# The second layer of 19 of 48 blocks as seven products of halves, two operand sums by accumulating DMA and two by VectorE

## The chip, the cores and the metric

The kernel runs on one core of a Trainium2 chip. Its time is the device time of one execution in microseconds (us), as a median over runs. One execution was also recorded by the hardware profiler; stretches and durations below come from that one.

## The reference

Two steps follow one another. First a filter along the sequence, in the frequency domain; then a two-layer network on every token, with a leaky activation whose slope for negative values is learned per hidden unit.

```python
# x: (8, 3008, 256); filt_r, filt_i: (1505, 256)
X = np.fft.rfft(x, axis=1)
Y = X * (filt_r + 1j * filt_i)[None]
y = np.fft.irfft(Y, n=3008, axis=1).reshape(24064, 256)
h = y @ w_in                                   # 256 -> 2048
g = np.maximum(h, 0.0) + alpha * np.minimum(h, 0.0)
out = g @ w_out                                # 2048 -> 256, float32
```

## The kernel before

**Blocks and steps.** The 24064 tokens are cut into 48 blocks: four times 12 blocks (two batches each), of which one has 384 tokens and the others 512. A block is worked in 16 steps, one for each tile of 128 hidden units. All engines are given their instructions in an order written out by hand; nothing is moved by a scheduler. Each engine takes its own instructions in that order and waits on semaphores for the others.

**First layer, `up(j)` (L446 to L456).** In step j TensorE multiplies two 128-row tiles of the transformed tokens `yT` by hidden tile j of `win_s`: two matmuls of 512 columns into PSUM tile `hps` (two buffers, each for a pair of hidden tiles). After each odd j ScalarE copies the pair as fp16 into `gtb` (L452), and VectorE makes the activation: two instructions `min(g, 0) * (alpha - 1)` into `m` (L455) and one sum `g + m` over the pair (L456). `gtb` is a ring of 17 pairs; a block fills eight.

**Second layer, `down(q)` (L465).** Beside the first layer of a block, TensorE does the second layer of the block before it: in each step a sixteenth of 64 matmuls, four of 256 columns, whose stationary operand is 128 hidden units x 128 tokens of `gtb` and whose moving operand is `wout_s`. 16 matmuls accumulate one tile of 128 tokens x 256 outputs in PSUM tile `op`; ScalarE evicts two of those at a time (L470) into `osb`, and SP's queue stores them. The last block is done by `finish` (L476), whose last 32 matmuls are 128 columns wide.

**The transform.** While a block of one batch is multiplied, the transform of a later batch is put between the steps in small pieces, by a plan that gives a step for each (`STEPS_A` to `STEPS_D`, in steps from the start of a batch's 96). `piece_a` is one matmul of 512 columns (L176); its result goes by `asb` to a DRAM scratch (`save_a`) and comes back turned (`turn_a`). `piece_b` (L196) has two matmuls of 256 columns, two multiplications by VectorE from PSUM (L199 `ww`, L200 `uu`), and two DMAs on POOL's queue that add `ww` into `uu` across the halves of the partitions (L202; `accum_op`). `piece_c` (L215) has two matmuls of 256 columns; its result `v` goes to DRAM (`turn_c`) and comes back as `zt`. `piece_d` has four matmuls of 94 columns into `yT` (L237). ScalarE evicts pieces a, c and d (L244). `BANKS` says which of two PSUM banks (`psF`) each piece takes. POOL's queue also loads x, with a cast from fp32 to fp16 (L138).

Batch 0 has a transform of its own at the start (`First`). The first 80 us hold it and the loading of the weights.

Of the kernel before, what the change touches and what calls it, by code (L numbers as in the profile page):

```python
# [16 lines left out]
NK1 = 24  # L17
# [6 lines left out]
    "010101010101010101010010101010101010110101010011001011101010010101011001010101010101010110101011"  # L24
    "001010110101010101010010010101010101010010101101010100110101010010101010101011011010101010101011"
    "010100101010110010101011010101010101001001010101010101001010110101010011010101001010101010101101"
    "10101010101010110101010101010101010101011010101010010101"
)
STEPS_A = (-84, -82, -74, -69, -67, -61, -59, -58, -55, -53, -52, -50, -47, -44, -41, -40)
STEPS_B = (-22, -16, -12, 1, 7, 16, 23, 29, 38, 45, 51, 56)  # L30
STEPS_C = (-1, 9, 20, 27, 34, 36, 42, 50, 54, 66, 70, 70)
STEPS_D = (89, 90, 90, 92, 93, 94, 96, 99, 101, 101, 103, 110, 114, 121, 127, 129)
# [44 lines left out]
def kernel(  # L77
# [22 lines left out]
    p_fft = ctx.enter_context(tc.tile_pool(name="p_fft", bufs=1))  # L100
    p_uw = ctx.enter_context(tc.tile_pool(name="p_uw", bufs=3))
# [3 lines left out]
    psO = ctx.enter_context(tc.tile_pool(name="psO", bufs=2, space=bass.MemoryType.PSUM))  # L105
# [21 lines left out]
    gtb = konst.tile([128, 17, 2, 512], FP16, name="gtb")  # L127
    twx_s = gtb[:, 14:17].rearrange("p a b c -> p (a b c)").rearrange("p (k m) -> p k m", m=128)
# [30 lines left out]

    class Fft:  # L160
        def __init__(self, b):
            self.b = b
            self.base = (b % 2) * NFFT
            self.px, self.uw = {}, {}

        def start_a(self):
            self.asb = p_fft.tile([96, NH, D], FP16, name="asb")
            self.at = p_fft.tile([128, NK1, D], FP16, name="at")

        def piece_a(self, i, evict, wide=False):  # L170
            if i == 0:
                self.start_a()
            xs = xc[(self.b, i // 4)]
            ps = bank(wide)
            o = (i % 4) * 512
            nc.tensor.matmul(ps[0:96], wf1_s, xs[:, o : o + 512], start=True, stop=True)  # L176
            evict(self.asb[:, 2 * i : 2 * i + 2].rearrange("p a d -> p (a d)"), ps[0:96])

        def save_a(self, c):
            s = slice(8 * c, 8 * c + 8)  # L180
            nc.sync.dma_start(out=a_dram[self.b, :, s], in_=self.asb[:, s])
# [23 lines left out]
        def piece_c(self, kp, evict, pv=None):  # L205
            if kp == 0:
                self.v = p_fft.tile([128, NK1, D], FP16, name="v")
                self.zt = p_fft.tile([96, NH, D], FP16, name="zt")
# [9 lines left out]
        def turn_c(self, q):  # L218
# [8 lines left out]
            if q == 3:  # L227
                for g in range(4):
                    s = slice(8 * g, 8 * g + 8)
                    nc.sync.dma_start(out=self.zt[:, s], in_=v_dram[self.b, :, s])  # L230

        def piece_d(self, i, evict, wide=False):
# [3 lines left out]
            for m in range(4):  # L236
                nc.tensor.matmul(ps[:, m], self.zt[:, 8 * g + 4 * mh + m, dh * 128 : dh * 128 + 128],  # L237
# [14 lines left out]
    class First(Fft):  # L252
        def __init__(self):
# [3 lines left out]
            self.zt = p_fft.tile([96, NH, D], FP16, name="zt")  # L257
            self.am = gtb[:, 0:6].rearrange("p a b c -> p (a b c)")
# [21 lines left out]
        def piece_b(self, kp):  # L280
# [6 lines left out]
            uw = gtb[:, 6 + kp % 8]  # L287
# [4 lines left out]
        def piece_c(self, kp, evict):  # L292
            uu, ww = self.uw.pop(kp)
            tw, tx = (t.rearrange("p k (q g e) -> p k g q e", q=4, e=4) for t in (twi_s, twx_s))
            pv = psO.tile([128, 2, D], FP32, name="op").rearrange("p k d -> p (k d)")
# [10 lines left out]
        def piece_t(self, i, evict, wide=False):  # L306
            pt = bank(wide)
            m = self.vm.rearrange("p (g m e) -> p g m e", m=96, e=4)
# [5 lines left out]
            evict(self.zt[:, 2 * i : 2 * i + 2].rearrange("p a d -> p (a d)"), pt[0:96])  # L314
# [34 lines left out]
    def warm(n):  # L349
        pw = psO.tile([128, 2, D], FP32, name="op")  # L350
# [12 lines left out]
    alp = psO.tile([128, 2, D], FP32, name="op")  # L363
# [70 lines left out]
    turn = [0]  # L434

    class Block:
        def __init__(self, p, t0, tn):
            self.p, self.t0, self.tn = p, t0, tn
            self.gts = []

        def up(self, j):
# [6 lines left out]
            if j % 2 == 1:  # L448
                g = gtb[:, turn[0] % 17]
                turn[0] += 1  # L450
                m = p_m.tile([128, 2, 512], FP16, name="m")
                nc.scalar.activation(g[:, :, 0:tn], self.hps[:, :, 0:tn], AF.Copy)  # L452
                for i in range(2):
                    a = alm_s[:, j - 1 + i : j + i]
                    nc.vector.tensor_scalar(m[:, i, 0:tn], g[:, i, 0:tn], 0.0, a, OP.min, OP.mult)  # L455
                nc.vector.tensor_add(g[:, :, 0:tn], g[:, :, 0:tn], m[:, :, 0:tn])  # L456
                self.gts += [g[:, 0], g[:, 1]]

        def down(self, q):
            n = self.tn // 128  # L460
            for w in range(n * q, n * (q + 1)):
                si, k = w // 16, w % 16
                if si % 2 == 0 and k == 0:
                    self.op = psO.tile([128, 2, D], FP32, name="op")
                nc.tensor.matmul(self.op[:, si % 2], self.gts[k][:, 128 * si : 128 * si + 128],  # L465
                                 wout_s[:, k], start=(k == 0), stop=(k == 15))
                if k == 15 and (si % 2 == 1 or si == n - 1):
                    m = si % 2 + 1
                    osb = p_osb.tile([128, 2, D], FP32, name="osb")
                    nc.scalar.activation(osb[:, 0:m], self.op[:, 0:m], AF.Copy)  # L470
                    for lane in range(m):
                        store(self.p, self.t0 + 128 * (si - m + 1 + lane), osb, lane)

        def finish(self):
            def down(acc, si, k, first, ca=0, cb=D):
                nc.tensor.matmul(acc, self.gts[k][:, 128 * si : 128 * si + 128], wout_s[:, k, ca:cb],  # L476
                                 start=first, stop=(k == 15), skip_group_check=True)

            op = psO.tile([128, 2, D], FP32, name="op")
# [11 lines left out]
            accs.insert(0, psO.tile([128, 2, D], FP32, name="op")[:, 0])  # L491
# [12 lines left out]
    def plan_fft(b, a0, ga, ta, b0, gap, add, lag, d0, quarters, x_at):  # L504
# [17 lines left out]
        for i in range(16):  # L522
            put(d0 + min(i, 4) + 2 * max(i - 4, 0), f.piece_d, i, on_act)

# [77 lines left out]
```

## Time and profile before

| | |
|---|---|
| median of 3 runs | 792.93 us (792.37 to 792.95) |
| the profiled execution's own time | 792.78 us |
| its span from first to last instruction | 791.0 us |
| TensorE matmuls (PE) | 772.4 us busy, 98% |
| VectorE (DVE) | 621.3 us, 79% |
| ScalarE (ACT) | 597.2 us, 76% |
| GpSimd (POOL) | 198.2 us, 25% |
| TensorE clock granted | 1.00 |
| DMA | 100.78 MB, 127 GB/s over the span |

The span is 1.8 us shorter than the execution's own time: what lies before the first and after the last instruction. Busy time of TensorE counts overlapping matmuls once; a matmul's duration contains its way through the array, so the pace of a stream is read from the distance of the starts. Engines are named as the profile names them: PE, PEld (weight loads), DVE, ACT, POOL and SP.

### The profile page before, as it was taken

The page shows a single profiled execution, that of the slowest core. Times are in us where ns is not written, and L with a number is a line of the kernel's source. Part 1 is how long each engine was busy: PE and PEld are TensorE (multiplying, and loading weights), DVE is VectorE, ACT ScalarE, POOL GpSimd, SP SyncE. Part 2 cuts the span into 40 slices and gives each one's busy share as a digit, 9 for nine tenths or more (in the row PEclk, how much of TensorE's full clock was granted, in tenths as well). Part 3 has the DMA queues.
Part 4 walks back from the last instruction along what each step waited for, and adds up shares of the span by engine and source line. Part 5 has one row for each costly group of instructions (what it writes and reads, how often), then busy time and mean ns, then how long its engine had stood idle before and what let it go on. Part 6 is the DMA issues. An engine that isn't in the chain of part 4 may idle for free.

```text
span 791.0 us, 16125 instructions
## 1 busy us (share of the span) xinstructions
PE 772.4 (98%) x5944; PEld 538.9 (68%) x5944; DVE 621.3 (79%) x1370; ACT 597.2 (76%) x839; POOL 198.2 (25%) x277
## 2 busy tenths in 40 slices
PE   7899999999999999999999999999999999999998
PEld 6756656666676666766667666766667766776666
DVE  4787985788788787887887878887888888777774
ACT  4788678878778887788768787788867777786663
POOL 7720541153123221341223321232212222000000
PEclk9999999999999999999999999999999999999999
DMA  9995557685676648574684757656484243511112
GB/s 192 188 211 165 109 121 170 191 175 117 140 184 114 126 113 205 107 146 103 147 195 79 141 120 152 170 104 128 112 188 113 61 91 74 134 41 35 41 41 54
DMA packets 102854, 100.78 MB, mean 127 GB/s; under 512 B 11432, under 2 KB 93112, under 8 KB 102648
## 3 DMA queue, kind: packets, MB, share of 16 engines
q1 hardware_dynamic: 79992, 69.52, 33.3%
q0 software_dynamic: 22640, 30.16, 24.3%
q8 instruction: 47, 0.77, 0.4%
q14 instruction: 31, 0.25, 0.1%
q10 hardware_dynamic: 144, 0.07, 0.0%
HBM read 56.06 MB, written 46.66 MB: 130 GB/s over the span
## 4 chain that ended last, share of the span: by engine, by line
PE 88%; DMA 3%; ACT 3%; DVE 2%; issue 1%; POOL 1%; SPq 0%; ACTq 0%; POOLq 0%; DVEq 0%
PE hps L446 38%; PE op L465 38%; PE psF L176 3%; PE psF L237 3%; PE psF L215 2%; PE psF L196 2%; ACT gtb L452 2%; DMA twf_s<-c_twf 1%; DMA uu<-ww 1%; PE op L476 1%; DMA filt_s<-in_filt_i_dram 1%; DMA zt<-v_dram 1%; PE psF L313 1%; DVE m L455 1%; ACT asb L244 1%
## 5 line engine op out<-in xcount | busy, mean ns | idle before, releaser
L452 ACT ACTIVATE gtb<-hps 128x1024 f16<-128x1024 f32 (+1 forms) x384 | 385.5, 1005 | 132.9 <-PE hps L446 128.1
L446 PE MATMUL hps<-yT,win_s 128*128 128x512 f16 (+1 forms) x1536 | 449.2, 374 | 0.4 <-ACT gtb L452 0.2
L465 PE MATMUL op<-wout_s,gtb 128*128 128x256 f16 x2944 | 444.0, 272 | 0.0
L465 PEld LDWEIGHTS <-gtb 128*128 128x128 f16 x2944 | 287.1, 98 | 188.0
L455 DVE TENSOR_SCALAR m<-gtb,alm_s 128x512 f16<-128x512 f16 (+1 forms) x768 | 236.2, 349 | 126.8 <-ACT gtb L452 124.0
L456 DVE TENSOR_TENSOR gtb<-gtb,m 128x1024 f16<-128x1024 f16 (+1 forms) x384 | 261.6, 681 | 19.8
L202 POOL DMA_DIRECT2D uu<-ww x168 | 140.7, 983 | 444.5 <-PE hps L446 310.7
L446 PEld LDWEIGHTS <-win_s 128*128 128x128 f16 x1536 | 145.2, 98 | 30.9 <-issue 3.1
L244 ACT ACTIVATE asb<-psF 96x512 f16<-96x512 f32 x112 | 66.2, 591 | 11.5 <-PE psF L176 11.4
L244 ACT ACTIVATE yT<-psF 128x376 f16<-128x376 f32 x120 | 57.1, 485 | 13.8 <-PE psF L237 13.3
L244 ACT ACTIVATE v<-psF 128x512 f16<-128x512 f32 x84 | 49.4, 595 | 10.9 <-PE psF L215 10.1
L199 DVE TENSOR_TENSOR ww<-psF,filts_s 128x512 f16<-128x512 f32 x84 | 57.4, 683 | 0.1
L200 DVE TENSOR_TENSOR uu<-psF,filt_s 128x512 f16<-128x512 f32 x84 | 57.1, 680 | 0.0
L470 ACT ACTIVATE osb<-op 128x512 f32<-128x512 f32 x94 | 54.9, 584 | 0.0
L138 POOL DMA_DIRECT2D xs<-in_x_dram x64 | 44.3, 974 | 18.9 <-PE psF L176 11.9
L176 PE MATMUL psF<-xs,wf_s 94*96 94x512 f16 x112 | 42.7, 381 | 1.5 <-ACT v L244 0.9
L237 PE MATMUL psF<-wi_s,zt 96*128 96x94 f16 x504 | 40.3, 205 | 2.4 <-DMA zt<-v_dram 1.5
L237 PEld LDWEIGHTS <-zt 96*128 96x128 f16 x512 | 34.3, 97 | 6.7 <-DMA zt<-v_dram 1.8
L215 PE MATMUL psF<-uu,twi_s 128*128 128x256 f16 x168 | 31.3, 273 | 2.2 <-DMA uu<-ww 1.0
L196 PE MATMUL psF<-at,twf_s 128*128 128x256 f16 x168 | 32.1, 273 | 0.4 <-ACT asb L244 0.3
L215 PEld LDWEIGHTS <-twi_s 128*128 128x128 f16 x168 | 15.7, 98 | 6.0 <-DMA uu<-ww 2.1
L196 PEld LDWEIGHTS <-twf_s 128*128 128x128 f16 x168 | 15.7, 98 | 2.9 <-DVE uu L200 0.6
(64 smaller groups left out, 190.6 us busy)
## 6 DMA issues: line engine op xcount, KB each, us to landing
out_dram<-osb SPq DMA_DIRECT2D x127, 128.0 KB
xs<-in_x_dram POOLq DMA_DIRECT2D x64, 188.0 KB, 5.6
a_dram<-asb SPq DMA_DIRECT2D x28, 384.0 KB
uu<-ww POOLq DMA_DIRECT2D x168, 64.0 KB, 3.0
v_dram<-v SPq DMA_DIRECT2D x112, 96.0 KB
zt<-v_dram SPq DMA_DIRECT2D x28, 384.0 KB
at<-a_dram SPq DMA_DIRECT2D x20, 384.0 KB
at<-a_dram SPq DMA_DIRECT2D x32, 96.0 KB
```

Of the source, the lines that this page charges most:

```text
L176: nc.tensor.matmul(ps[0:96], wf1_s, xs[:, o : o + 512], start=True, stop=True)
L196: nc.tensor.matmul(px[:, kh], twf_s[:, k1, 64:192], self.at[:, k1], start=True, stop=True)
L199: nc.vector.tensor_mul(ww, px, filts_s[:, 2 * kp : 2 * kp + 2])
L202: nc.gpsimd.dma_start(out=uu[o : o + 64], in_=ww[64 - o : 128 - o], accum_op=OP.add)
L215: nc.tensor.matmul(pv[:, kh], twi_s[:, k1], u[:, kh], start=u is us[0], stop=u is us[-1])
L237: nc.tensor.matmul(ps[:, m], self.zt[:, 8 * g + 4 * mh + m, dh * 128 : dh * 128 + 128], wi3_s, start=True, stop=True)
L244: nc.scalar.activation(o, i, AF.Copy)
L446: nc.tensor.matmul(self.hps[:, j % 2, 0:tn], win_s[:, kt, j * 128 : (j + 1) * 128], yT[:, kt, self.t0 : self.t0 + tn], start=(kt == 0), st ...
L452: nc.scalar.activation(g[:, :, 0:tn], self.hps[:, :, 0:tn], AF.Copy)
L455: nc.vector.tensor_scalar(m[:, i, 0:tn], g[:, i, 0:tn], 0.0, a, OP.min, OP.mult)
L456: nc.vector.tensor_add(g[:, :, 0:tn], g[:, :, 0:tn], m[:, :, 0:tn])
L465: nc.tensor.matmul(self.op[:, si % 2], self.gts[k][:, 128 * si : 128 * si + 128], wout_s[:, k], start=(k == 0), stop=(k == 15))
```

## The change

The second layer of a block is a product of G (512 tokens x 2048 hidden units) and W (2048 x 256). In 19 blocks, `FAST`, both are cut into halves: G into a11, a12, a21, a22 (first index: half of the tokens; second: even or odd hidden tiles), W into b11 to b22 (even or odd hidden tiles; half of the outputs). Instead of eight products of halves there are seven, by Strassen's scheme in Winograd's form. Fast are the even blocks from 12 to 40 (in the text also "0, 2, 4 mod 6", by their place in a batch's six blocks), and 42 to 45.

- Four sums of W's halves (`n1`, `n2`, `t3`, `t4`) are made once by VectorE (`combine`, five instructions at steps 130 to 142).
- Each fast block needs four sums of G's halves. VectorE makes `z1 = a21 + a22` and `z2 = z1 + a11` in two parts each; POOL's queue issues two DMAs of 512 KB from SBUF to SBUF that add a11 into a21 and z2 into a12, in place. `SUMS` (`TAIL` for blocks 40 and later) gives for each the step, counted from the block's first.
- The products are 7 x 16 matmuls of 128 columns, seven in each step. ScalarE takes five partial results of 256 columns out of PSUM, and VectorE makes the block's outputs of them with two fp32 instructions (put into the next step by `late`).
- `gtb` becomes two buffers of one block each (16 pairs in place of 17). PSUM tiles `op` are taken in turn by `obank`. The second layer follows the first 16 steps later (`LAG`), by a running count of the work done.
- `asb` and `zt` are cut in quarters (two and three buffers); the fourth quarter of `zt` is loaded after `piece_d` 3 (`load_z(3)`). `BANKS` and the four lists of steps have new values.

```diff
+FAST = frozenset([n for n in range(12,42) if n%6 in (0,2,4)]+[42,43,44,45])
+SUMS = ((8, 1, 0), (12, 2, 0), (17, 1, 1), (17, 2, 1), (17, 3, None), (25, 4, None))
+TAIL = ((17, 1, 0), (18, 1, 1), (18, 3, None), (18, 2, 0), (18, 2, 1), (22, 4, None))
+LAG = 16
-STEPS_B = (-22, -16, -12, 1, 7, 16, 23, 29, 38, 45, 51, 56)
+STEPS_B = (-22, -16, -15, 6, 7, 17, 25, 28, 35, 41, 51, 59)
...
-    gtb = konst.tile([128, 17, 2, 512], FP16, name="gtb")
+    tw_s = konst.tile([128, 4, 8, 128], FP16, name="tw_s")
+    ss = konst.tile([128, 2, 8, 256], FP16, name="ss")
+    gtb = konst.tile([128, 2, 8192], FP16, name="gtb")
...
     class Block:
+            self.fast = n in FAST
+            self.g = gtb[:, n % 2]
+            self.q = self.g.rearrange("p (l h k c) -> p l h k c", l=2, h=2, k=8)
...
+        def pair(self, k):
+            if self.fast:
+                return self.q[:, :, :, k]
+            return self.g.rearrange("p (k l c) -> p k l c", k=8, l=2)[:, k, :, 0 : self.tn]
...
+        def sums(self, w, h):
+            k = slice(0, 8) if h is None else slice(4 * h, 4 * h + 4)
+            a11, a21, a12, a22 = (self.q[:, l, t, k] for l in range(2) for t in range(2))
+            z1, z2 = ss[:, 0, k], ss[:, 1, k]
+            if w == 1:
+                nc.vector.tensor_add(z1, a21, a22)
+            elif w == 2:
+                nc.vector.tensor_add(z2, z1, a11)
+            elif w == 3:
+                nc.gpsimd.dma_start(out=a21, in_=a11, accum_op=OP.add)
+            else:
+                nc.gpsimd.dma_start(out=a12, in_=z2, accum_op=OP.add)
...
+        def seven(self):
...
+            br, bq = obank(), obank()
+            r, q, q2 = br[:, 0], bq[:, 0], bq[:, 1]
+
+            def product(acc, x, b, first):
+                self.begun += 1
+                for k in range(8):
+                    for i in range(2):
+                        nc.tensor.matmul(acc[:, 128 * i : 128 * i + 128], x[:, k, 128 * i : 128 * i + 128], b[:, k],
+                                         start=first and k + i == 0, stop=k == 7, skip_group_check=True)
+                        yield 1 / 112
...
+            yield from product(r, a11, b11, True)
+            s1 = p_osb.tile([128, 2, D], FP32, name="osb")
+            nc.scalar.activation(s1[:, 0], r, AF.Copy)
+            yield from product(q, a12, b21, True)
+            yield from product(q2, a22, t4, True)
+            o2 = p_osb.tile([128, 2, D], FP32, name="osb")
+            nc.scalar.activation(o2[:, :, 0:128], halves(q2), AF.Copy, scale=-1.0)
+            yield from product(r, ss[:, 1], n2, False)
+            nc.scalar.activation(s1[:, 1], r, AF.Copy)
+            yield from product(q2, ss[:, 0], n1, True)
+            nc.scalar.activation(o2[:, :, 128:256], halves(q2), AF.Copy, scale=-1.0)
+            yield from product(r, a21, t3, False)
+            u3 = p_sn.tile([128, 256], FP32, name="sn")
+            nc.scalar.activation(u3, r, AF.Copy)
+            o = o2.rearrange("p i (h c) -> p i h c", h=2)
+            late.append((nc.vector.tensor_sub, (o, o, halves(u3).unsqueeze(2).to_broadcast([128, 2, 2, 128]))))
...
+            yield from product(q2, a12, b22, False)
+            o1 = p_osb.tile([128, 2, D], FP32, name="osb")
+            late.append((nc.vector.tensor_add, (o1.rearrange("p i (h c) -> p h i c", h=2),
+                                                *(t.rearrange("p h (i c) -> p h i c", i=2) for t in (bq, s1)))))
...
+        put(p + STEPS_D[3] + 2, f.load_z, 3)
...
         for j in range(16):
+            step = 16 * n + j
+            flush()
+            for b, w, h in ahead.pop(step, ()):
+                b.sums(w, h)
             for fn, args in plan.pop(step, ()):
                 fn(*args)
             blk.up(j)
-            if prev is not None:
-                prev.down(j)
+            while todo and done < (step - LAG) / 16:
+                try:
+                    done += next(todo[0])
+                except StopIteration:
+                    todo.pop(0)
+        todo.append(blk.items())
```

## The prediction

> **What bounds the kernel now.** I read the share of busy time first, then the stretch in the middle, then the groups, then single timelines. The page, its busy times and the engines' shares of the chain that ended last:
>
> ```profile
> PE 772.4 (98%) x5944; PEld 538.9 (68%) x5944; DVE 621.3 (79%) x1370; ACT 597.2 (76%) x839; POOL 198.2 (25%) x277
> PE 88%; DMA 3%; ACT 3%; DVE 2%; issue 1%; POOL 1%; SPq 0%; ACTq 0%; POOLq 0%; DVEq 0%
> ```
>
> The windows view of 250 to 690 us (busy time of PE, PEld, DVE, ACT, POOL, then granted clock, share of the DMA engines, GB/s):
>
> ```profile
> 250.00:690.00 440.00, 440.00 (x3279) 305.69 (x3277) 356.63 (x797) 343.33 (x476) 106.10 (x136) 1.00 0.59 128
> ```
>
> In those 440 us TensorE is never idle, at full clock, and 88% of the chain of work that ended last is TensorE. VectorE is busy for 81%, ScalarE for 78%. Busy matmuls are not yet matmuls at their pace, so I looked at starts in the timeline: four L465 matmuls of 256 columns and two L446 matmuls of 512 repeat every 0.87 us, which is 4 x 109 ns + 2 x 216 ns. No time is lost between them. Whatever takes columns off TensorE therefore shortens the span, until another engine is late.
>
> The price of a narrow matmul is in the last microseconds, where `finish` runs 48 matmuls of 256 columns and then 32 of 128, each with its own weights (timeline of PE, 780 us on; then the groups of that stretch):
>
> ```profile
> 780.32 5.40 PE L476 MATMUL op<-wout_s,gtb 128*128 128x256 f16 x48
> 785.56 1.95 PE L476 MATMUL hps<-wout_s,gtb 128*128 128x128 f16 x32
> ```
>
> ```profile
> L476 PEld LDWEIGHTS <-gtb 128*128 128x128 f16 x80 | 6.6, 98 | 0.6
> L476 PE MATMUL hps<-wout_s,gtb 128*128 128x128 f16 x32 | 1.9, 219 | 0.0
> ```
>
> The last of 48 lasts 0.273, so the others start (5.40 - 0.273) / 47 = 109 ns apart; of the 32, (1.95 - 0.219) / 31 = 56 ns. A weight load lasts 98 ns, but the loads overlap: new weights every 56 ns do not slow the stream.
>
> **TensorE.** A fast block drops 64 matmuls of 256 columns, 64 x 109 = 6.98 us, and issues 7 x 16 = 112 of 128 columns, 112 x 56 = 6.27 us. That is 0.70 us per block, 13.4 us over 19 blocks. The order is written by hand, and the built program has 2128 = 19 x 112 of them, so the change does what it says. Bounds for one narrow matmul are 56 ns and the 98 ns of its load; I take 56, from the same shape and weights.
>
> The Trainium skill (TensorE: Matmul & The Clock Gate, "Back-to-back issue gap") speaks against this change: it gives about 81 ns per matmul for streams of weight load and 128-column matmul, and keeps 56 ns for matmuls without loads. By that rule, as an estimate, a block would take 112 x 81 = 9.07 us, 2.1 us more than now, and the kernel about 833 us. The 32 rows above do have a load each, and run at 56.
>
> **VectorE.** Its own pace is seen where work was queued for it (timeline of DVE):
>
> ```profile
> 330.85 0.68 DVE L199 TENSOR_TENSOR ww<-psF,filts_s 128x512 f16<-128x512 f32 x1
> 331.45 0.68 DVE L200 TENSOR_TENSOR uu<-psF,filt_s 128x512 f16<-128x512 f32 x1
> 332.05 0.60 DVE L455 TENSOR_SCALAR m<-gtb,alm_s 128x512 f16<-128x512 f16 x2
> 332.69 0.69 DVE L456 TENSOR_TENSOR gtb<-gtb,m 128x1024 f16<-128x1024 f16 x1
> ```
>
> Starts are 0.08 us closer than durations. A pair of hidden tiles costs 0.64 + 0.61 = 1.25 us, a block 10.0 us; a `piece_b` costs 1.20 us, 14.4 us per batch. A fast block adds four fp16 sums of 1024 (L456's shape, 0.61 each) and two fp32 sums of 512, which the trace does not have; nearest are L199 and L200 at 0.60 (the bound above is 1.13, L289's pace with 1024 from PSUM, below it nothing is won). I take 0.60: 2.44 + 1.20 = 3.64 us. Six blocks (5.875 of full size) with three fast ones are then 5.875 x 10.0 + 14.4 + 3 x 3.64 = 84.1 us. TensorE needs 5.875 x 13.89 + 11.5 for the transform - 2.1 = 91.0 us. VectorE goes to 92%: full, not yet late. With both fp32 sums at the bound it is 87.3. The pair's add in chunks of 256 costs nothing by the 768-element form in two chunks (558 ns against 692 for 1024, the same price per element). The five `combine` steps, 3 us once, fit beside blocks 8.
>
> Blocks 42 to 45 are fast in a row and have no `piece_b`: TensorE 13.2 us a block, VectorE 10.0 + 3.64 = 13.7. There it is late by 0.5 us a block.
>
> **ScalarE.** Two evictions of 512 (0.49 us apart) become five of 256 (about 0.27): 0.4 us a block, beside 76%. Each narrow eviction must end before a product writes the same PSUM columns; a product of 0.9 us and two or three steps' first-layer matmuls (0.43 each) lie between, about 2 us against at most one pair eviction (0.92), a transform eviction (0.48) and itself. Nothing charged.
>
> **The entry of a fast block.** Its first product needs the eighth pair after 14 matmuls. That pair is complete 2.9 us after its last first-layer matmul starts; TensorE has 2.65 us of work in between without transform pieces. After every fast block in 12 to 38 the plan has two pieces (0.22 each) there, so nothing is lost; after 40 to 45 about 0.2 us each.
>
> **The two accumulating DMAs.** 128 partitions x 4096 B each, 38 of them. The trace has only 64 KB ones, and 512 KB loads that cast:
>
> ```profile
> xs<-in_x_dram POOLq DMA_DIRECT2D x64, 188.0 KB, 5.6
> uu<-ww POOLq DMA_DIRECT2D x168, 64.0 KB, 3.0
> win_s<-in_moe_w_in_dram POOLq DMA_DIRECT2D x2, 512.0 KB, 6.5
> wout_s<-in_moe_w_out_dram POOLq DMA_DIRECT2D x2, 512.0 KB, 9.5
> ```
>
> In the packet records a 1024 B packet of L202 takes 0.102 us, and a 4096 B packet of the casting loads, which like an accumulate move two bytes in for one out, 0.32. Eight packets per engine are 2.6 us (3.3 at four times 0.102). The first packet of L202 starts 1.4 us after POOL's issue. So 4.3 to 5.0 us from issue to landing alone, and up to 6.5, win_s's, with the engines as full as there (0.95). Their share goes from 0.59 to about 0.76 (two of 2.6 us in every two blocks of 31 us add 0.17).
>
> When must they land? Take the fast block's first second-layer step as 0. The eighth pair is done at 2.2 us. The a21 sum waits in POOL's queue for the second half of z1; the a12 sum waits for product two (about 5 us) and, in POOL's order, for the `uu` DMAs of a `piece_b` whose VectorE work comes after the sums. Products six and seven start at 10.1 and 11.9 us plus the pieces between (1.3 to 2.0 us). Blocks 0, 2, 4 mod 6: a12 is issued at 6.2, 7.4, 7.4 and needed at 13.8, 13.2, 13.5. The tightest margin is 5.8 us; a21 has at least 6.2. At 5 to 6.5 us little is late; I charge 1 us in all. In blocks 43 to 45 VectorE takes the old block's sum, half of z1 and a pair first, so a21 is issued near 5.9, needed at 10.1: 4.2 us of margin. With the DMA share at 0.14 there, 0.3 to 1 us late each; a12's packets follow in the same queue. With VectorE's 0.5 us, which falls in the same waits, and the entries I charge 3 us for the end.
>
> Queued behind the two on POOL are `uu` DMAs, whose `piece_c` comes 10 or more steps later (9 us), and loads of x used a batch later: free. SP's moved `load_z(3)` waits for `piece_d` 3 and has 13 us before its first use; the two `asb` buffers have 5 us at batch 1, where 1 us would be lost once if the save is late.
>
> **Sum.** 792.8 (span 791.0 and 1.8 around it; the median is 792.93, so the two agree) - 13.4 + 1 + 3 = **783.4 us**.
>
> **Rivals.** *Late sums* (the other side). The accumulates take longer than I think, and TensorE waits before products six and seven, with everything behind it in order. After the 3 us at the end, 10.4 us are left for 15 blocks; ten of these have margins near 6 us, so it decides where an accumulate lands 7 us after issue. At 8 us the margins are exceeded by 2.2, 1.9 and 0.4 us in five blocks each, 22 us, and the end loses some 10: 811 us. For it: wout_s's 9.5 and a largest xs landing of 13 us; against: both at the fullest times, and the 0.102 us of L202's packets. 15%.
>
> *VectorE becomes the bound.* If a fast block costs it 2.3 us more than I count, 91 us per six blocks are reached; half of that already gives waits at block ends, where the eighth pair is awaited. 4 to 8 us go: 789. 12%.
>
> *Loads pace narrow matmuls* at 98 ns: 112 x 98 = 10.98, + 4.0 us x 19: 869 us. Only the mean of 98 speaks for it, the 56 ns starts against. 3%. The skill's 81 ns is the milder form of it.
>
> **Numbers.** Forecast (779 to 787) 63%; late sums 15%; VectorE 12%; loads 3%; gain and waits cancel 5%; unnamed loss 2%. About 0.2% (1.6 us) is what a measurement can tell. Faster 75%, same 5%, slower 20%. The range starts at the full 13.4 (779) and reaches past no change to mildly late sums, 797; beyond lie the heavier late sums and the loads.
>
> **What would show it.** Right: the 128-column matmuls start 56 ns apart; VectorE near 90%; waits before the new line's sixth product only in the last blocks; accumulates landing in 5 to 6.5 us. Wrong: waits of TensorE on the gtb DMAs of a microsecond per fast block, VectorE without idle time and TensorE waiting for L456's successor, or narrow matmuls 80 ns or more apart.

## The result, and the profile after

| | before | after |
|---|---|---|
| median | 792.65 us (791.91 to 792.95, 4 runs) | 830.51 us (827.82 to 832.93, 4 runs) |
| ratio | | 1.048, interval 1.0441 to 1.0516 |
| profiled execution | 792.78 us, span 791.0 | 831.85 us, span 830.1 |

The change costs 38 us where 9.4 were forecast as a gain. The page after, with the busy times and the engines' shares of the chain:

```profile
PE 774.8 (93%) x6856; PEld 545.0 (66%) x6856; DVE 685.1 (83%) x1489; ACT 607.7 (73%) x896; POOL 232.8 (28%) x315
...
PE 59%; DMA 19%; DVE 11%; ACT 5%; issue 3%; POOL 2%; DVEq 0%; SPq 0%; POOLq 0%; ACTq 0%
```

TensorE's share of the chain falls from 88% to 59%, that of the DMA rises from 3% to 19%. The same stretch of the windows view as before:

```profile
250.00:690.00 440.00, 412.14 (x3702) 287.85 (x3700) 377.55 (x824) 331.43 (x494) 132.59 (x166) 0.99 0.71 152
```

TensorE was never idle here; now it is idle for 28 of 440 us. The waits of PE by line (us in total, times, longest) and one wait of ScalarE name the releasers:

```profile
PE op L537 <- DMA gtb<-ss: 24.6, 16, 3.7
PE op L537 <- DMA gtb<-gtb: 7.8, 7, 1.5
PE psF L190 <- ACT asb L260: 3.6, 2, 3.1
```

```profile
ACT asb L260 <- DMA a_dram<-asb: 3.8, 1, 3.8
```

L537 is the line of all products. The two DMAs are the accumulates: gtb<-ss (a12, L504) and gtb<-gtb (a21, L502). Products six and seven wait 32.4 us for them. Their rows among the DMA issues (KB, median us to landing) beside the two of before:

```profile
xs<-in_x_dram POOLq DMA_DIRECT2D x64, 188.0 KB, 6.7
...
uu<-ww POOLq DMA_DIRECT2D x168, 64.0 KB, 3.0
...
gtb<-gtb POOLq DMA_DIRECT2D x19, 512.0 KB, 5.9
gtb<-ss POOLq DMA_DIRECT2D x19, 512.0 KB, 7.2
```

The a12 sum takes 5.3 to 10.2 us, a21 4.5 to 8.1. One of the waits, in block 30, in the timeline of PE:

```profile
569.93 0.44 PE L537 MATMUL op<-tw_s,gtb 128*128 128x128 f16 x5
574.06 0.28 PE L537 MATMUL op<-wout_s,gtb 128*128 128x128 f16 x2 [3.68 <-DMA gtb<-ss]
574.18 0.33 PE L253 MATMUL psF<-wi_s,zt 96*128 96x94 f16 x4
574.35 0.60 PE L478 MATMUL hps<-yT,win_s 128*128 128x512 f16 x2
574.79 0.66 PE L537 MATMUL op<-wout_s,gtb 128*128 128x128 f16 x7
575.24 1.06 PE L478 MATMUL hps<-yT,win_s 128*128 128x512 f16 x2
```

Product six ends at 570.4, product seven begins at 574.06, and everything behind it in TensorE's order stands meanwhile. After the wait two L478 matmuls last 1.06 us instead of 0.60. The windows view of the wait and of what follows shows why (eighth column the granted clock):

```profile
570.00:574.00 4.00, 0.38 (x6) 0.20 (x4) 2.90 (x6) 0.76 (x2) 1.16 (x2) 1.00 0.68 158
574.00:578.00 4.00, 3.94 (x28) 2.65 (x29) 1.31 (x3) 1.95 (x3) 0.49 (x1) 0.64 0.51 101
```

The clock records have four such stretches in the middle of the run, each 3.413 us at 0.5. Each costs about 1.7 us, and each begins within 1 us of the end of a wait of 3.1 to 3.7 us. The length agrees with the Trainium skill (TensorE: Matmul & The Clock Gate, "Part 1: The HAM clock gate"), which gives a free-running window of 3413 ns and halves the clock after at least one idle window. An idle stretch of that length was not needed here: three of the four waits were 3.15 to 3.32 us, and waits of 2.3 and 2.6 us did the same in experiments 18 and 16.

The balance: I added, over all matmuls from about 80 us on (behind the first transform and the loading of the weights), the time from start to start beyond a matmul's own pace (216, 109, 56 ns and so on). That is 10.1 us before and 62.1 after, half-clock stretches included. 791.0 - 13.4 + (62.1 - 10.1) = 829.6; the span is 830.1. So the saving is there in full, and 52 us of lost time stand against it; 38.5 of the 62.1 lie between two matmuls of products.

### The profile page after: what moved, and what is told of

It reads as the page before. It is cut to its first block, busy times and chain, and to the rows that moved or that the text cites. A ratio compares the mean times of both kernels' runs of the same rounds, so it can differ in the third digit from the quotient of the medians.

```text
span 830.1 us, 17980 instructions
## 1 busy us (share of the span) xinstructions
PE 774.8 (93%) x6856; PEld 545.0 (66%) x6856; DVE 685.1 (83%) x1489; ACT 607.7 (73%) x896; POOL 232.8 (28%) x315
## 4 chain that ended last, share of the span: by engine, by line
PE 59%; DMA 19%; DVE 11%; ACT 5%; issue 3%; POOL 2%; DVEq 0%; SPq 0%; POOLq 0%; ACTq 0%
PE hps L478 25%; PE op L515 18%; DMA gtb<-ss 15%; PE op L537 6%; DVE m L489 3%; ACT gtb L486 3%; PE psF L190 2%; DVE gtb L490 2%; PE psF L228 2%; PE psF L253 2%; PE psF L210 1%; DVE ww L213 1%; DVE ss L498 1%; POOL uu L216 1%; DVE uu L214 1%
## 5 line engine op out<-in xcount | busy, mean ns | idle before, releaser
L478 PE MATMUL hps<-yT,win_s 128*128 128x512 f16 (+1 forms) x1536 | 452.4, 377 | 0.4 <-ACT gtb L486 0.2
L489 DVE TENSOR_SCALAR m<-gtb,alm_s 128x512 f16<-128x512 f16 (+1 forms) x768 | 234.4, 347 | 102.9 <-ACT gtb L486 101.6
L490 DVE TENSOR_TENSOR gtb<-gtb,m 128x1024 f16<-128x1024 f16 (+1 forms) x384 | 261.6, 681 | 17.4 <-DVE m L489 0.5
L515 PE MATMUL op<-wout_s,gtb 128*128 128x256 f16 x1728 | 262.7, 273 | 0.0
L515 PEld LDWEIGHTS <-gtb 128*128 128x128 f16 x1728 | 168.8, 98 | 114.5 <-issue 1.2
L537 PEld LDWEIGHTS <-gtb 128*128 128x128 f16 x1520 | 104.5, 99 | 85.3 <-DMA gtb<-ss 28.6
L478 PEld LDWEIGHTS <-win_s 128*128 128x128 f16 x1536 | 138.1, 99 | 31.8 <-issue 8.6
L537 PE MATMUL op<-wout_s,gtb 128*128 128x128 f16 x912 | 78.3, 223 | 25.5 <-DMA gtb<-ss 24.6
L260 ACT ACTIVATE v<-psF 128x512 f16<-128x512 f32 x84 | 50.1, 596 | 16.2 <-PE psF L228 15.7
L537 PE MATMUL op<-tw_s,gtb 128*128 128x128 f16 x608 | 52.6, 219 | 7.8 <-DMA gtb<-gtb 7.8
L502 POOL DMA_DIRECT2D gtb<-gtb x19 | 19.8, 1042 | 135.2 <-DVE ss L498 81.7
L213 DVE TENSOR_TENSOR ww<-psF,filts_s 128x512 f16<-128x512 f32 x84 | 57.4, 683 | 0.0
L214 DVE TENSOR_TENSOR uu<-psF,filt_s 128x512 f16<-128x512 f32 x84 | 57.1, 680 | 0.0
L537 PEld LDWEIGHTS <-ss 128*128 128x128 f16 x608 | 42.6, 98 | 20.9
L537 PE MATMUL op<-tw_s,ss 128*128 128x128 f16 x608 | 52.5, 219 | 0.0
L148 POOL DMA_DIRECT2D xs<-in_x_dram x64 | 46.8, 1092 | 19.0 <-PE psF L190 12.7
```

The costliest lines, as they stand in the source:

```text
L213: nc.vector.tensor_mul(ww, px, filts_s[:, 2 * kp : 2 * kp + 2])
L214: nc.vector.tensor_mul(uu, px, filt_s[:, 2 * kp : 2 * kp + 2])
L260: nc.scalar.activation(o, i, AF.Copy)
L478: nc.tensor.matmul(self.hps[:, j % 2, 0:tn], win_s[:, kt, j * 128 : (j + 1) * 128], yT[:, kt, self.t0 : self.t0 + tn], start=(kt == 0), st ...
L489: nc.vector.tensor_scalar(ms[:, i], g[:, i], 0.0, a, OP.min, OP.mult)
L490: nc.vector.tensor_add(g, g, ms)
```

## The experiments

The ratios are to the kernel before, run beside each. "Lost" is the sum just defined.

**1. Without the accumulates.**

```diff
-            elif w == 3:
-                nc.gpsimd.dma_start(out=a21, in_=a11, accum_op=OP.add)
-            else:
-                nc.gpsimd.dma_start(out=a12, in_=z2, accum_op=OP.add)
```

> Both accumulating DMAs are left out, so products six and seven use a21 and a12 as they are; all else is as in the changed kernel. Theory (late landings): the 37 us that TensorE loses inside the fast second layer, and most of the half-clock stretches after the long waits, go: 786 to 793 us. Rival (VectorE and the new plan of steps hold TensorE up): 810 us or more remains. If the 128-column matmuls themselves were the loss, 825 or more.

791.28 us (787.92 to 793.48, 10 runs), ratio 0.998 (0.9965 to 0.9994). The two DMAs cost 39 of the 830.5 us. Inside the products 0.4 us are lost instead of 38.5. But 17.9 us are lost in all, 7.8 more than before, in the profiled execution (787.92 us, the shortest of the ten: 13.4 - 7.8 = 5.6 us gained, by the spans 4.9). By the medians the kernel gains only 1.6 us (792.92 beside it) where the products save 13.4: something else in the change also costs.

**2. The a12 sum written where nobody waits for it.** The products multiply by an a12 that isn't summed.

```diff
-                nc.gpsimd.dma_start(out=a12, in_=z2, accum_op=OP.add)
+                nc.gpsimd.dma_start(out=a11, in_=z2, accum_op=OP.add)
```

> The second accumulate adds z2 into a11 in place of a12: the same 512 KB over the same queue and engines at nearly the same time, but nothing on TensorE reads a11 any more. Theory (TensorE waits for the landing): the waits before product seven go, some 25 us and two or three half-clock stretches of 1.7 us: 798 to 805 us; those before product six stay. Rival (the traffic itself slows everything else): 820 us or more.

812.6 us (809.44 to 817.93), ratio 1.0254 (1.0206 to 1.0303). Its waits by PE:

```profile
PE op L537 <- DMA gtb<-gtb: 10.5, 6, 3.5
```

The wait for a12 is gone and 18 us with it, but 21 us of the DMAs' 39 stay. The a21 sum is late 10.5 us in six blocks, and the clock records have 13.7 us at 0.5 before the end, another 6.8 us. One thing clouds the reading: writing to a11 makes this DMA wait on POOL until the a21 sum, which reads a11, has landed, so its own landing of 5.5 us is that of a DMA with no a21 packets ahead of it.

**3. The a12 sum by VectorE.**

```diff
-SUMS = (..., (25, 4, None))
+SUMS = (..., (23, 4, 0), (25, 4, 1))
...
-                nc.gpsimd.dma_start(out=a12, in_=z2, accum_op=OP.add)
+                nc.vector.tensor_add(a12, a12, z2)
```

> The sum a12 + z2 by VectorE in two parts of 0.61 us in place of the DMA; one DMA per fast block is left. Theory: the waits before product seven go, the first DMA meets less traffic, and VectorE has room for 1.2 us more per fast block until block 40 (88 of 91 us per six blocks), not in the last blocks: 795 to 803 us. Rival (VectorE is already the bound): 815 us or more.

805.57 us (804.48 to 808.37), ratio 1.0164 (1.0141 to 1.0187). 25 us better than the change, 14 us over the kernel without accumulates. 5.6 us of waits for a21 are left (4 of them), with one half-clock stretch. PE waits 8.0 us for VectorE, for gtb sums and `uu`, where it was 2.1 without the accumulates. How the rest of the 14 us divides isn't shown.

**4. Both sums by GpSimd's own adder.**

```diff
-                nc.gpsimd.dma_start(out=a21, in_=a11, accum_op=OP.add)
+                nc.gpsimd.tensor_add(a21, a21, a11)
-                nc.gpsimd.dma_start(out=a12, in_=z2, accum_op=OP.add)
+                nc.gpsimd.tensor_add(a12, a12, z2)
```

> Both sums as additions by GpSimd in place of DMAs. Its copies of 768 columns took 1.07 ns an element, so a sum of 2048 takes 2.2 us, or 4.4 if two operands cost double: shorter than 6 to 7 us of a DMA. Theory: little wait is left, 788 to 800 us. Rival: GpSimd and VectorE slow each other down, or GpSimd at over 3 ns an element holds up the uu DMAs behind it: 830 us or more.

941.08 us (938.42 to 941.9), ratio 1.1862 (1.184 to 1.1884). The groups by form:

```profile
L504 POOL TENSOR_TENSOR gtb<-gtb,ss 128x2048 f16<-128x2048 f16 x19 | 87.5, 4603 | 3.6 <-DVE ss L500 3.6
...
L489 DVE TENSOR_SCALAR m<-gtb,alm_s 128x512 f16<-128x512 f16 x704 | 317.4, 493 | 49.4 <-ACT gtb L486 48.3
...
L500 DVE TENSOR_TENSOR ss<-ss,gtb 128x1024 f16<-128x1024 f16 x38 | 45.0, 1196 | 0.5
```

One of the sums in the timeline of POOL and DVE:

```profile
303.68 4.49 POOL L502 TENSOR_TENSOR gtb<-gtb 128x2048 f16<-128x2048 f16 x1 [5.07 <-DVE ss L498]
304.17 4.42 DVE L489 TENSOR_SCALAR m<-gtb,alm_s 128x512 f16<-128x512 f16 x2
308.69 0.69 DVE L490 TENSOR_TENSOR gtb<-gtb,m 128x1024 f16<-128x1024 f16 x1
```

A sum takes 4.5 to 4.6 us, no longer than a quick accumulate, yet this is the slowest kernel of all, because VectorE stands still beside it. The means of 493 and 1196 ns (350 and 687 in the change) mix two kinds: 34 operations of L489, L490 and L500 that met an add took 2.9 to 9.7 us and ended 0.1 to 0.6 us behind its end, and those clear of the adds keep their old times. L213 and L214, which read PSUM, keep 683 and 680 ns inside an add too. The 38 adds take 173 us, and the kernel is 150 us over that of experiment 1. The Trainium skill (GPSIMD Engine Reference, "1. Specifications") says that the two engines share SBUF interfaces, with contention when VectorE runs a two-port mode or has two SBUF inputs. L490 and L500 have two SBUF inputs, as that would have it; whether L489 runs in such a mode the trace does not say.

**5. Accumulates of half the size.** Only k 0 to 3 of each sum is added.

```diff
-                nc.gpsimd.dma_start(out=a21, in_=a11, accum_op=OP.add)
+                nc.gpsimd.dma_start(out=a21[:, 0:4], in_=a11[:, 0:4], accum_op=OP.add)
...
-                nc.gpsimd.dma_start(out=a12, in_=z2, accum_op=OP.add)
+                nc.gpsimd.dma_start(out=a12[:, 0:4], in_=z2[:, 0:4], accum_op=OP.add)
```

> Each accumulate carries only its first four hidden tiles (256 KB); the other half of both sums is left out. Everything is issued at the same places. Theory (the landing is too late by its own transfer and by what shares queue and engines with it): each landing is shorter by 1.3 us of its own packets and the second by up to as much again behind the first; of some 37 us of waits 25 to 35 go: 796 to 808 us. Rival (the fixed part of the DMA or the late issue is what hurts): little changes, 820 us or more.

802.02 us (801.11 to 809.68), ratio 1.0136 (1.0077 to 1.0195). Landing falls from 5.9 and 7.2 us to 4.8 and 5.8, not to half, and the waits to 5.5 + 1.7 us. 256 KB take away 1.1 and 1.4 us. Of the full landing only 2.6 us are the accumulate's own packets (eight of 0.328 us per engine); the larger part is the time to the first packet (1.4 to 1.5 us after the issue with nothing ahead of it) and standing among other transfers. The waits fall from 32.4 to 7.2 us, because the margins lie in between.

**6. The a12 sum issued earlier.** The first two products change places, and pieces B leave the stretch.

```diff
-SUMS = (..., (25, 4, None))
+SUMS = (..., (20, 4, None))
-STEPS_B = (-22, -16, -15, 6, 7, 17, 25, 28, 35, 41, 51, 59)
+STEPS_B = (-22, -18, -11, 6, 7, 21, 25, 28, 35, 41, 53, 59)
+            yield from product(q, a12, b21, True)
             yield from product(r, a11, b11, True)
...
-            yield from product(q, a12, b21, True)
```

> The two first products change places, so a12 is free 2 us sooner, and the second accumulate stands right behind the first on POOL's queue, ahead of the uu DMAs; four steps of piece_b move for that (17 to 21, 51 to 53, 80 to 78, 81 to 85 of 96). Same sums, same sizes. Theory (the margin is what counts): issue near 2.5 us after the first product's start in place of 6, landing near 9 to 10, seventh product at 11.9: most waits before products six and seven go, 797 to 808 us. Rival (transfers slow down whatever waits beside them): 820 us or more, the waits moving to piece_c.

821.5 us (819.04 to 828.12), ratio 1.0369 (1.0319 to 1.0419). The waits for the two DMAs fall from 32.4 to 10.4 us, but the time only by 9: with the products swapped the first one needs at once the PSUM tile that the block before has only just filled, and 10.6 us of waits for evictions (L457, 6.3; L520, 4.3) take their place.

**7. Both sums by VectorE.**

```diff
-SUMS = (..., (17, 3, None), (25, 4, None))
+SUMS = (..., (19, 3, 0), (21, 3, 1), (23, 4, 0), (25, 4, 1))
...
-                nc.gpsimd.dma_start(out=a21, in_=a11, accum_op=OP.add)
+                nc.vector.tensor_add(a21, a21, a11)
...
-                nc.gpsimd.dma_start(out=a12, in_=z2, accum_op=OP.add)
+                nc.vector.tensor_add(a12, a12, z2)
```

> All four operand sums by VectorE, none by DMA: 2.44 us more of it per fast block, 84.1 + 7.3 = 91.4 us per six blocks against TensorE's 91.0, and 16 against 13.2 us a block at the end. Theory: VectorE is the bound now, waits move from the DMAs to L490 and the sums; about 795 to 812 us, better than the DMAs all the same. Rival (VectorE has more room than counted): under 793.

814.92 us (813.56 to 819.21), ratio 1.0282 (1.0248 to 1.0316). No DMA is waited for, VectorE is busy 723.7 us, and PE waits 6.7 us for `uu` before L210 and 6.6 for L490's sums before L537. VectorE has free room for neither sum: the first cost waits for it in experiment 3, and the second adds 9 us by the medians.

**8. Experiment 6 with SP's queue cleared** (loads of x later, batch 2 one step earlier).

```diff
-    plan_fft(2, 66, 2, 97, 109, 4.5, 8, 12, 187, 4, (110, 114, 118, 122))
+    plan_fft(2, 65, 2, 97, 109, 4.5, 8, 12, 187, 4, (110, 114, 118, 122))
-                put(p + (6, 10, 16, 20)[c], ...)
+                put(p + (6, 10, 28, 33)[c], ...)
```

> As the early issue, and two loads of x per batch move from steps 16 and 20 to 28 and 33, out of the way of the first fast block's accumulates; batch 2's piece_a and saves come one step sooner, so that its second save stands ahead of the zt loads on SP's queue. Theory: 3 to 6 us less than with the early issue alone, 792 to 803 us, and no wait of ScalarE for a_dram near 135 us. Rival: no difference.

820.5 us (819.8 to 821.04), ratio 1.0342 (1.0323 to 1.0362): 1 us under experiment 6, within that one's spread. The stretch from 100 to 150 us, where the change loses 7.9 us and the kernel before 3.9, is back at 3.7. So the 3.8 us wait for an `asb` tile at 135 us was a matter of order on SP: `save_a(1)` stood behind loads of `zt` that wait for `v_dram` (the moved loads of x come later than 150 us). Experiment 6's new waits stay.

**9. The plan and the buffers alone.**

```diff
-FAST = frozenset([n for n in range(12,42) if n%6 in (0,2,4)]+[42,43,44,45])
+FAST = frozenset()
```

> The changed kernel with no fast block: all 48 second layers in the old form (no sums, no accumulates), but with the new buffers, the new steps of the transform and the new lag. Theory (8 us of the loss are the reworked plan and its smaller buffers, whatever the products): 797 to 803 us, TensorE's waits at 120 to 140 us and in the transform's pieces as in the run without accumulates. Rival (the plan costs nothing by itself, what was left without accumulates came from VectorE's two sums and two late steps): 792 to 795 us.

802.17 us (800.06 to 804.09), ratio 1.0109 (1.0094 to 1.0124). Without any product of halves the new steps and buffers cost 9 us: 20.2 us are lost instead of 10.1, about 5 of it at the wait of 135 us and the half clock behind it. Experiment 1, the same plan with the products and without the accumulates, is 10.9 us faster: most of the 13.4 us is there when nobody waits for the sums.

**10. Wider margins.** No swap; pieces B clear of the sums, a12 at step 22, 18 blocks, with experiment 8's SP order.

```diff
-STEPS_B = (-22, -16, -15, 6, 7, 17, 25, 28, 35, 41, 51, 59)
+STEPS_B = (-22, -10, -8, 6, 7, 22, 25, 28, 35, 41, 54, 59)
-FAST = frozenset([n for n in range(12,42) if n%6 in (0,2,4)]+[42,43,44,45])
+FAST = frozenset(range(12, 48, 2))
```

> Products in their first order. The second accumulate stands at step 22 in place of 25, and four piece_b move behind it (17 to 22, 51 to 54, 80 to 86, 81 to 88), so that no uu DMA stands ahead of either accumulate; the loads of x go to steps 28 and 33 in place of 16 and 20; batch 2's piece_a one step sooner; fast are the even blocks 12 to 46 (18 of them), none next to another. Theory: issue of the second near 4 us after the first product's start, landing near 11, needed at 11.9: waits for DMAs under 8 us in all, 786 to 796 us, level with the kernel before or a little faster. Rival (the accumulates are slower the more stands beside them, whatever the order): 805 us or more.

816.59 us (812.85 to 818.68), ratio 1.0298 (1.0276 to 1.0319). The waits of PE:

```profile
PE psF L253 <- DVE uu L214: 9.8, 10, 1.5
PE psF L190 <- DVE uu L214: 8.6, 5, 3.5
...
PE op L537 <- DMA gtb<-gtb: 1.3, 1, 1.3
...
PE op L537 <- DMA gtb<-ss: 1.1, 1, 1.1
```

The sums are in time, 2.4 us of waits instead of 32.4. In their place pieces of the transform stand behind a moved piece B, which holds its PSUM bank until VectorE has come to it.

**11 and 12. Banks chosen by how long they are held, then the same without the accumulates.**

```diff
-        return psF[int(next(order))].tile([128, 512], FP32, name="psF")
+        i = int(next(order))
+        if now[0] >= 0:
+            i = int(free[1] < free[0])
+            free[i] = max(free[i], now[0]) + hold    # 5 steps for a piece B, 2 for others
+        return psF[i].tile([128, 512], FP32, name="psF")
```

> This is the kernel with the wider margins (both accumulates in time, pieces B of the transform moved) with one thing more: inside the loop over the blocks, the transform's pieces take the PSUM bank that comes free first by a simple count (a piece B holds its bank for 5 steps, any other piece for 2) in place of the written list of banks, which was made for other steps. Theory 1 (the 817 us of the wider margins came from pieces that stood behind a piece B on the same bank: 9.8, 8.6 and 2.4 us of waits for VectorE's uu, and the half clock of 2 x 5 us after them): these waits fall to some 3 us in all, the waits for the accumulated sums stay at 1 to 4 us, and the time is 788 to 798 us, level with the kernel before or under it. Rival (VectorE is simply late in this kernel, whatever the bank): the waits for uu stay at 15 us or more, or come back as waits of the up products, and the time is 808 to 818 us.

> The same kernel with both accumulating DMAs of the sums left out, so the products of the 18 blocks multiply by sums that aren't complete. It tells what of the time left is due to the accumulates in any way. Theory 1: 784 to 794 us, 2 to 6 us under the one with them. Rival (VectorE late): within 2 us of the one with them, both over 805 us.

807.45 us (805.23 to 809.87), ratio 1.0191 (1.0177 to 1.0204), and 804.56 (802.89 to 806.59), ratio 1.0148 (1.0128 to 1.0169). The sums are in time as the first theory has it (1.9 us of waits), and the two kernels lie 2.9 us apart by the medians, with ranges that overlap: with wide margins the accumulates cost that instead of 39 us. But both times are 10 us over its figures and near the rivals'. D pieces still wait 9.7 us for VectorE's `uu`, behind two pieces B that hold a bank each.

**13, 14 and 15. The pieces B at -22, -20, -18; the same with the change's 19 blocks; and without any.**

```diff
-STEPS_B = (-22, -10, -8, 6, 7, 22, 25, 28, 35, 41, 54, 59)
+STEPS_B = (-22, -20, -18, 6, 7, 22, 25, 28, 35, 41, 54, 59)
```

> The kernel with the banks by hold, with two things more: the three early pieces B stand at steps -22, -20 and -18 instead of -22, -10 and -8, clear of the D pieces at -7 to -4 and of the sums' accumulates, and the counted choice of banks begins with block 12 (the written list serves before it, as in the change). Theory 1 (the 803 us span of the kernel with the banks by hold is 12 blocks of waits for banks that lie where the pieces were put: 10.7 us of D pieces behind B pieces, 7.9 us of B behind C in batches 1 and 2): both go, the time is 785 to 792 us, under the kernel before. Rival (VectorE is late in any placement, and each move only shifts its wait): 798 to 808 us.

> The same with the 19 blocks of the change, blocks 42 to 45 among them, and the change's order of the sums at the end. Theory 1: 785 to 793 us, within 2 us of the kernel with 18 blocks (one block more saves 0.7 us, blocks 43 and 45 follow a block of seven products directly and may wait 1 to 3 us for their sums). Rival: as for the kernel with 18 blocks, 798 to 808 us.

> The same placement without a block of seven products: all second layers as the eight products of the kernel before, no sums, no accumulates of them. It separates what the placement gains from what the products gain. Theory 1 (the products gain 0.7 us a block, some 13 us, and the placement costs 3 to 8 us against the kernel before's): 796 to 802 us. Rival (the new placement is itself the gain, and the products bring nothing net): within 3 us of the kernel with 19 blocks.

805.91 us (803.85 to 811.2), ratio 1.0174 (1.0147 to 1.02); 811.35 (809.22 to 812.27), ratio 1.0228 (1.0214 to 1.0242); 803.96 (802.19 to 806.51), ratio 1.0142 (1.0126 to 1.0158). My theory fell. In the first of the three:

```profile
PE op L545 <- DVE gtb L498: 6.4, 4, 2.1
PE op L545 <- DMA gtb<-ss: 5.0, 6, 1.5
...
PE op L545 <- DMA gtb<-gtb: 3.2, 3, 1.6
...
PE psF L261 <- DVE uu L222: 2.6, 3, 2.3
```

(L545 is the line of the products here, L498 that of the pair's add.) The banks are nearly free now, and the wait has moved to the products: for the last pair, and for both accumulates. By the sum of lost time, the 18 blocks save 12.6 us and lose 37.2 - 19.6 = 17.6 us against the same placement without them (with 18 blocks the profiled execution, 809.43 us, lies above the median). By the medians it is 2.0 us behind that one, within their spread, and with 19 blocks 7.4 us behind. The products gain nothing here.

**16 and 17. The steps and banks of the kernel before, put back; 12 blocks where those steps issue few pieces B; then none.**

```diff
-FAST = frozenset([n for n in range(12,42) if n%6 in (0,2,4)]+[42,43,44,45])
+FAST = frozenset(n for n in range(12, 48) if n % 6 in (1, 3))
```

> The change with the steps and the list of banks of the kernel before, put back unaltered (only batch 2 starts its pieces one step earlier), and seven products in 12 blocks instead of 19: those whose sums fall into stretches of that plan in which few pieces B of the transform are issued (13, 15, 19, 21 and so on to 43 and 45, where n mod 6 is 1 or 3). The second accumulate is issued at step 22 instead of 25. Theory 1 (the loss of the change is in its plan and in the late second accumulate, and the products themselves gain 0.7 us a block): 12 x 0.70 = 8.4 us less than the same kernel without them, and 786 to 792 us against 793 of the kernel before. Rival (every block of seven products pays 1 to 2 us of waits wherever its sums stand, as the last placement suggests): 796 to 806 us, over the kernel without them.

> The same without a block of seven products: steps and banks of the kernel before, with the buffers of the change (two of asb, three of zt, two of gtb). It prices those buffers. Theory 1 (the 9 us of the change's plan came from its steps): 793 to 797 us. Rival (they came from the smaller buffers): 799 to 803 us.

804.71 us (802.42 to 808.03), ratio 1.0151 (1.0127 to 1.0174), and 799.71 (798.43 to 800.6), ratio 1.0084 (1.007 to 1.0098). The second says that most of experiment 9's 9 us are not the new steps: with the old ones the rest of the change still costs 7 us. That is the smaller buffers, but also `combine`, the second layer's order by a running count, the later `load_z(3)` and batch 2's earlier start, which no run takes apart. In the first, TensorE hardly waits for the sums, but 7.4 us for another transfer:

```profile
PE psF L210 <- DMA at<-a_dram: 7.4, 3, 4.3
...
PE op L537 <- DMA gtb<-ss: 1.4, 2, 0.8
```

**18. The first piece B of a batch 5 steps later.**

```diff
-STEPS_B = (-22, -16, -12, 1, ...)
+STEPS_B = (-17, -16, -12, 1, ...)
```

> The old plan with 12 blocks of seven products, its first piece B of a batch at step -17 instead of -22, 4 us later. In the kernel it comes from, that piece waited in blocks with n mod 6 = 3 for the load of at (7.4 us in 3 waits, up to 4.3), which has to share the DMA engines with the two accumulates issued 5 and 10 steps behind it. Theory 1 (this is the last wait that belongs to the products; beyond it they gain 0.7 us a block): the wait falls under 2 us, and the time is 792 to 798 us, under the same plan without products (799.7) and level with the kernel before or above it by what the buffers cost. Rival (the wait comes back at another place): 801 to 807 us.

799.97 us (798.34 to 801.86), ratio 1.0086 (1.0071 to 1.0101).

```profile
PE op L537 <- DMA gtb<-gtb: 8.6, 4, 3.0
...
PE op L537 <- DMA gtb<-ss: 1.1, 2, 1.0
```

The wait for `at` went, and the a21 sum became late instead. Both waits are in the blocks with n mod 6 = 3, where the trace has four loads of `at` (384 KB each) issued from 3.2 us before to 0.1 us after the a21 sum (512 KB): whichever is needed first is late. Over both kernels the a21 sum lands in 9.2 to 10.9 us in these blocks, and in 4.6 to 6.0 us in the eight that have no load of `at` beside it (n mod 6 = 1, and 39 and 45, behind the last such load). Block 39 has the place in the plan that block 33 has, and as much on POOL's queue while its sum is under way (0.8 to 0.9 MB in both); without `at` its sum lands in 5.8 and 6.0 us instead of 9.2 and 9.5. The eight blocks lose 0.3 us or less in their products. 8.4 us saved and 26.3 - 16.2 = 10.1 us lost leave the two kernels of this plan level (799.97 and 799.71).

## Why the prediction was wrong

The step that failed is the landing time in "The two accumulating DMAs": 5 to 6.5 us, with 1 us charged for blocks 12 to 40. The issue times stand. From a fast block's first product on, block 20 issues a12 at 6.05 us, and its seventh product could start at 11.85: 5.8 us, the margin as worked out. (In blocks 0 mod 6 it is 6.4 to 6.8, where I had 7.6.) The landing is the term that was mis-sized: 4.5 to 4.6 us with little in its way, as estimated (a21 in blocks 36, 44, 45; a 4096 B packet takes 0.328 us, 0.32 was estimated), but for a12 a median of 7.2 and up to 10.2 us, for a21 up to 8.1. My upper bound was a load's median at a full DMA; an accumulate issued behind `uu` DMAs, the a21 sum or loads of x waits for their packets in the same queue, and shares each engine with the saves of q1. In block 20 the packet records have a12's first packet 1.9 us after its issue, behind those of `uu`, and then its own, of 0.33 us and more, in turn with q1's of 0.17 to 0.36. I used the share of 0.76 (0.71 measured from 250 to 690 us) as a note, not as a stretch of the landing. Blocks 12 to 40 lose 34 us in their products where 1 was charged, blocks 42 to 45 5 us where 3 were. That company on the engines makes a landing long is shown by blocks 33 and 39 of experiments 16 and 18; how much of the change's own excess is the queue and how much the engines, no run separates.

The rival *late sums* is what happened. Its decision point, 7 us, was passed by a12. Its price, 811 at 8 us, came out too low, mostly because it left out the half clock after long waits (three times 1.7 us) and what the second failed step cost.

The second failed step is "two `asb` buffers ... 1 us would be lost once". The change without its products costs 9 us (experiment 9), and 7 under the old steps (experiment 17). One wait was of the kind named, a late save, in batch 2 instead of batch 1. It was 3.8 us long and cost a half-clock stretch. How the rest divides among buffers, order and steps isn't shown.

Right were:
- The narrow matmul: of 1821 starts that follow directly on another such matmul, 1743 come 55 to 57 ns behind it. The Trainium skill's 81 ns (TensorE: Matmul & The Clock Gate, "Back-to-back issue gap") does not hold for this stream. By it the kernel would have taken 833 us, near what was measured, and for another reason: experiment 1 has the same matmuls and takes 791.
- VectorE's prices, here in the groups by form:

```profile
L490 DVE TENSOR_TENSOR gtb<-gtb,m 128x1024 f16<-128x1024 f16 x352 | 243.7, 692 | 15.2 <-DVE m L489 0.5
...
L498 DVE TENSOR_TENSOR ss<-gtb 128x1024 f16<-128x1024 f16 x38 | 26.1, 688 | 0.8
...
L457 DVE TENSOR_TENSOR osb<-osb,sn 128x512 f32<-128x512 f32 x19 | 13.0, 684 | 0.0
L457 DVE TENSOR_TENSOR osb<-op,osb 128x512 f32<-128x512 f32 x19 | 13.0, 683 | 0.0
```

 The fp16 sums cost what L490 costs, and the fp32 sums what L213 (683 ns) does. The rival *VectorE becomes the bound* did not happen in the change, but experiments 3 and 7 show how near it is.
- ScalarE's narrow evictions (378 to 391 ns; 1.0 us of waits for L557), and the entries of the fast blocks, which lose nothing.
- The rival *loads pace narrow matmuls* is out by the 56 ns.

The 5% for "gain and waits cancel" describes the kernel that is left when the accumulates are taken away.

## What to carry to other kernels

A transfer's landing in a kernel is not its landing alone: read who else has packets in the same queue and on the same engines between its issue and its deadline, and take the longest landing of that company, not its median, where the margin is 6 us and the wait is in TensorE's order. A saving of 0.7 us a block has to be priced with everything that is moved to make room for it; here that took 9 us before the first product was run. A full plan has no free place: taken from the sums, the wait went to PSUM banks, to the load of `at`, to the last pair, and back to the sums; so compare each version with its own plan without the change, not only with the kernel before.

No version tried beats the kernel before with all its work done; the best is level with its own plan, 0.9% behind. Whether the eight blocks that lost 0.3 us or less, with buffers that cost less, would gain their 5.6 us was not tried.

## What the runs showed of the hardware that was not expected

- All four waits of TensorE of 3.1 us or more were followed by 3.413 us at half clock, about 1.7 us on top of the wait. In other runs waits of 2.3 and 2.6 us were too (experiments 18 and 16), and one of 2.3 us was not (experiment 15).
- An accumulate of half the size lands only 1.1 to 1.4 us sooner (4.8 and 5.8 against 5.9 and 7.2 us).
- GpSimd's add of 128x2048 fp16 takes 4.5 to 4.6 us, and VectorE's operations on SBUF alone that meet it do not slow down but stand until it is done (34 of them, 2.9 to 9.7 us instead of 0.3 to 0.7); L213 and L214, which read PSUM, keep their times.
- The same 512 KB accumulate lands in 4.6 to 6.0 us, and in 9.2 to 10.9 us with 1.5 MB of loads on SP's queue, another queue than its own, issued 3.2 us before it and later (experiments 16 and 18).
